# Reordering loads, transposes, stores and evacuations in the first three token tiles of a fused retention and gated-MLP kernel

## The chip, the cores and the metric

The kernel runs on one core of a Trainium2 chip. A core has five engines that run side by side and meet at semaphores: TensorE (PE in the profile; PEld is its weight load), VectorE (DVE), ScalarE (ACT), GpSimd (POOL) and SyncE (SP), which here only issues transfers. The metric is the device time of one execution in microseconds, as the median of several runs. The kernel before takes 303.74 us (three runs, 303.12 to 304.06). Times inside an execution come from a profile of it, whose span is 302.9 us.

## The reference

Two layers follow each other. The first is a retention layer: attention without softmax, whose scores decay with distance. Batch and heads are 8 each, the sequence has 576 tokens, the head dimension is 64. The second takes the 4608 tokens of 512 features through a layer of 2048.

```python
scores = q @ k.T / sqrt(64)                       # per batch and head
gamma  = 1 - 2 ** (-5 - head)
D[i, j] = gamma ** (i - j) if i >= j else 0
ret    = (scores * D) @ v                         # 8 x 8 x 576 x 64
x      = ret.transpose(0, 2, 1, 3).reshape(4608, 512)
h      = x @ w_in                                 # 4608 x 2048
g      = h * cos(h)
out    = g @ w_out                                # 4608 x 512, float32
```

## The kernel before

Tokens are handled in *pairs* of two 128-token tiles; there are 18 pairs of 256 tokens, numbered 0 to 17. For a pair the kernel loads q, k and v (1.5 MB), multiplies q and k by their decay factors and casts them (`prep`), turns them so that the head dimension lies on the partitions (`transposes`), and works out the retention in chunks: the part inside a chunk from masked scores, and the rest from a running state per head, which `states` sums up and `carry` moves on. The result goes from PSUM to `xT`, which feeds the second layer.

The second layer runs in ten *stages* n: widths 512, 256, 256, and then seven times 512 tokens. Stage 0 needs pairs 0 and 1, stage 1 pair 2, stage 2 pair 3, stage 3 pairs 4 and 5, stage 4 pairs 6 and 7. `mm1` is x @ w_in with the cosine, `mm2` is the second product. From stage 3 on, the second product is done with seven products in the place of eight (`mm2_seven`), for which sums of weights (`w_sums`) and of g (`g_sum`) are made on VectorE and GpSimd. The retention of later pairs is woven into the products of earlier stages.

Every load, DMA transpose and row store is issued from one queue, in program order:

```python
LD = 3                       # buffers for loaded q, k and v
def load(G, names="qkv", gate=None):
    for name in names:
        f = ld.tile([P, H, 2, D], F32, tag="f" + name, name=f"f{name}")
        for rows, ys, b, s0, cnt in parts:
            i = nc.sync.dma_start(f[rows, :, ys, :]..., src[b, :, s0 : s0 + cnt, :]...)
            if gate is not None:                  # the first transfer waits for a weight piece
                fence(i, gate, "weights first"); gate = None

def transposes(G, y, bank=None):
    qks, vb, qkT = tiles["a", G]
    if bank is None:                              # by DMA, from the same queue
        nc.sync.dma_start(qkT[:, y], qks[:, y]..., transpose=True)
        return
    ...                                           # pair 2: eight TensorE transposes
    nc.scalar.copy(qkT[:, y]..., ps[:, :, : HG * P])
```

The cast of v is put into the queue of one engine at the point where `prep` is called:

```python
def prep(G, y, engines=None, copy_v=None):
    ...
    scaled(eng, 0, tiles["fq", G], gq)            # eng is GpSimd unless told otherwise
    scaled(eng, 1, tiles["fk", G], gk)
    if copy_v is None:
        copy_v = nc.scalar.copy if G > 9 else nc.gpsimd.tensor_copy
    if copy_v:
        copy_v(vb[:, :, y], tiles["fv", G][:, :, y])
```

The store of each finished 128-token row tile s also drives the loading of later pairs. Up to stage 2 this goes through `bring` and a table, after that by a count:

```python
def mm2(n, tsi, et):
    ...
    if et == ET - 1:
        nc.scalar.copy(ot, ps)
        nc.sync.dma_start(out[s * P : (s + 1) * P, :], ot)
        feed(s)

loaded, prepared, transposed = 5, 4, 4
def bring(G):                                     # load ahead, prepare up to pair G, transpose
    while loaded < min(NP, G + LD, prepared // 2 + LD): load(loaded); loaded += 1
    while prepared < 2 * G + 2: prep_next()
    while transposed < prepared: transposes(...); transposed += 1

def feed(s):
    n, r = divmod(s - starts[S7] // P, 4)         # S7 = 3
    if n < 0:
        if s in when: bring(when[s])
        return
    while loaded < min(NP, prepared // 2 + LD): load(loaded); loaded += 1
    upto = starts[S7] // P + 12 + 4 * n + ((0, 0, 2, 4) if n else (0, 0, 2, 2))[r]
    while prepared < min(NG, upto): prep_next()
    while transposed < prepared: transposes(...); transposed += 1

when = {0: 3, 1: 4, 3: 5, 4: 6, 6: 7}             # a further bring(8) stands in stage 3
```

A retention ends with a copy of two halves from PSUM to `xT`. `done()` does both on ScalarE; `done(*both)`, with `both = (nc.scalar.copy, nc.vector.tensor_copy)`, does one on each engine. `begin` starts a pair's retention with its state part, `end` adds the rest and calls `done`. The second product of stages 0 to 2 is a list of matmuls into which such steps are put by index; stage 0's list before:

```python
todo = [(34 + 3 * i, w_sums(x, e, e + 4)) ...six of them...] + [
    (40, lambda: prep(2, 1, nc.vector, False)),
    (43, lambda: transposes(2, 0, "a")),
    (46, lambda: transposes(2, 1, "b")),
    (48, values2),                                # v of pair 2 and v_odd, both on ScalarE
    (50, lambda: at_once(*ready(2, states_bank=("n", "st")))),   # scores, states, masks
    (61, lambda: begin(2, ("n", "st"))),
    (64, lambda: end(both)),
]
```

Of the kernel before, what the change touches and what calls it, by code (L numbers as in the profile page):

```python
# [17 lines left out]
def kernel(  # L18
# [42 lines left out]
    LD = 3  # L61
# [49 lines left out]
    def half(x):  # L111
        return slice(x * HP, x * HP + HP)

    def load(G, names="qkv", gate=None):

        parts = []
        if G < FINE:
            t, end = G * 2 * P, (G + 1) * 2 * P
            while t < end:
                b, s0 = divmod(t, S)  # L120
                cnt = min(end - t, S - s0)
                p0 = (t - G * 2 * P) // 2
                parts.append((slice(p0, p0 + cnt // 2), slice(0, 2), b, s0, cnt))
                t += cnt
        else:
            for y in range(2):
                t0 = (2 * G + y) * P
                step = HP if (2 * G + y) % PER == MIX else P
                for p0 in range(0, P, step):
                    b, s0 = divmod(t0 + p0, S)  # L130
                    parts.append((slice(p0, p0 + step), slice(y, y + 1), b, s0, step))
        for name in names:
            src = {"q": q, "k": k, "v": v}[name]
            f = ld.tile([P, H, 2, D], F32, tag="f" + name, name=f"f{name}")
            for rows, ys, b, s0, cnt in parts:
                n = ys.stop - ys.start
                i = nc.sync.dma_start(  # L137
                    f[rows, :, ys, :].rearrange("p h r d -> p h (r d)"),
                    src[b, :, s0 : s0 + cnt, :].rearrange("h (p r) d -> p h (r d)", r=n),
                )  # L140
                if gate is not None:
                    fence(i, gate, "weights first")
                    gate = None
            tiles["f" + name, G] = f
# [28 lines left out]
            fv = tiles["fv", G]  # L173
            copy_v(vb[:, :, y], fv[:, :, y])  # L174

    def transposes(G, y, bank=None):
        qks, vb, qkT = tiles["a", G]
        if bank is None:
            nc.sync.dma_start(  # L179
                qkT[:, y], qks[:, y].rearrange("s m h d -> s (m h d)"), transpose=True  # L180
            )
            return
        ps = psum.tile([P, 2, 1024], BF16, tag=bank, name="tr")
        for m in range(2):
            for hg in range(HG):
                nc.tensor.transpose(
                    ps[:, m, hg * P : hg * P + P],
                    qks[:, y, m, 2 * hg : 2 * hg + 2, :].rearrange("s h d -> s (h d)"),
                    ident,
                )  # L190
        nc.scalar.copy(
            qkT[:, y].rearrange("p (m b) i -> p m (b i)", m=2), ps[:, :, : HG * P]
        )

    def key_transposes(G, bank):
        qks, vb, qkT = tiles["a", G]
# [27 lines left out]
    def blocks_of(G, y, hg):  # L224
        return slice(2 * hg, 2 * hg + 2) if G < FINE else slice(y * HG + hg, y * HG + hg + 1)

    def scores(G, banks="ab", idle=0, mid=lambda: None):

# [3 lines left out]
        for (y, ys), bank in zip(planes, banks):  # L234
            ps = psum.tile([P, 2, 2 * HG, HP], F32, tag=bank, name="sc")
            if idle:
                warm(ps[:, 0].rearrange("p b i -> p (b i)"), idle)
            ret = retp.tile([P, 2, 2 * HG, HP], BF16, tag="ret", name="ret")
            for u in range(2) if y is None else (y,):
                yq = slice(u, u + 1) if y is None else ys  # L240
                tiles["ret", G, u] = ret
                for hg in range(HG):
                    for x in range(2):
                        for he in range(2):
                            nc.tensor.matmul(  # L245
                                ps[half(x), he, blocks_of(G, u, hg), :],
                                lhsT=qkT[half(he), u, HG + hg, half(x)],
                                rhs=queries(G, he, hg, x, yq),
                                start=True,
                                stop=True,  # L250
                            )

            def masked(y=y, ps=ps, ret=ret):
                if y is None:
                    shape, by = [P, 2, 2 * HG, HP], tri.unsqueeze(1)
                    by = by.unsqueeze(1).to_broadcast(shape)
                    nc.vector.tensor_tensor(out=ret, in0=ps, in1=by, op=ALU.mult)  # L257
                    return
                shape = "p a (b r) i -> p (a b) (r i)"
                by = (mixed if G == 2 else tri2)[y].rearrange("p r i -> p (r i)")  # L260
                nc.vector.tensor_tensor(  # L261
                    out=ret.rearrange(shape, r=2),
                    in0=ps.rearrange(shape, r=2),
                    in1=by.unsqueeze(1).to_broadcast([P, H, P]),
                    op=ALU.mult,
                )

            masks.append(masked)
            if len(masks) == 1:
                mid()  # L270
        return masks

    def steps(G):
# [182 lines left out]
        for masked in masks:  # L456
            masked()

    def carry(G, bank):
        add, copy = states(due(G), bank)  # L460
        add()
        copy()

# [40 lines left out]
    def mm2(n, tsi, et):  # L504
# [11 lines left out]
        )  # L516
        if et == ET - 1:
            s = starts[n] // P + tsi
            ot = op.tile([P, DM], F32, tag="oabcd"[1 + s % 4], name="ot")
            nc.scalar.copy(ot, ps)  # L520
            nc.sync.dma_start(out[s * P : (s + 1) * P, :], ot)  # L521
            feed(s)

    E2 = ET // 2
    N2 = DM // 2
# [193 lines left out]
                    r0 = starts[n] + 256 + j * P  # L719
                    nc.sync.dma_start(out[r0 : r0 + P, N2 + c0 : N2 + c1], u22[:, j, c0:c1])  # L720

    loaded, prepared, transposed = 5, 4, 4
    open_ = []

    def begin(G, bank="m"):
        run, done = retention(G, bank)
# [10 lines left out]
        prep(prepared // 2, prepared % 2, **kw)  # L737
        prepared += 1

    def bring(G):  # L740

        nonlocal loaded, transposed
        while loaded < min(NP, G + LD, prepared // 2 + LD):
            load(loaded)
            loaded += 1
        while prepared < 2 * G + 2:
            prep_next()
        while transposed < prepared:
            transposes(transposed // 2, transposed % 2)
            transposed += 1  # L750

    def feed(s):

        nonlocal loaded, transposed
        n, r = divmod(s - starts[S7] // P, 4)
        if n < 0:
            if s in when:
                bring(when[s])
            return
        while loaded < min(NP, prepared // 2 + LD):  # L760
            load(loaded)
            loaded += 1
# [4 lines left out]
            transposes(transposed // 2, transposed % 2)  # L767
            transposed += 1

    when = {0: 3, 1: 4, 3: 5, 4: 6, 6: 7}  # L770

    G4 = 4
    fq4 = gp.tile([P, H, G4, D], F32, tag="gT", name="fq4")
# [121 lines left out]
    nc.gpsimd.tensor_copy(tiles["a", 1][1], tiles["fv", 1])  # L895
    w_dma += [load_w_in(e, e + 512) for e in (1024, 1536)]
    w_dma += [load_w_out(e, e + 4) for e in range(0, ET, 4)]
    load(2, gate=w_dma[5])
    load(3)
    load(4)  # L900
    plane = key_transposes(1, "m")
    plane(0)
    run, done = retention(0, ("n", "st"))
    run("cross", True)
    plane(1)
    masks1 = scores(1, mid=lambda: (run("own"), run("same"), done()))
    for masked in masks1:
        masked()
    add, copy = states(due(1), "m")
    add()  # L910
    copy()
# [7 lines left out]
        nc.gpsimd.tensor_copy(mixed[r], tri2[r])  # L919
        nc.gpsimd.memset(mixed[r][:QP, :, QP:], 0.0)  # L920
    prep(2, 0, copy_v=False)
    prepared = transposed = 6
    run1, done1 = retention(1, ("n", "st"))

    def values2():
        fv, vb = tiles["fv", 2], tiles["a", 2][1]
        nc.scalar.copy(vb, fv)
        nc.scalar.copy(v_odd[QP:HP], fv[QP:HP])

    late = []  # L930
    for n, w in enumerate(widths):

        if n in (0, 3):
# [1 line left out]
            if n == 3:  # L935
                order_.sort()
            else:
                order_[1:3] = order_[2:0:-1]
            blocks = [(et, h * 256, 256) for h, et in order_]
        else:  # L940
            m = 1024 // w
# [4 lines left out]
        for i, (et, c0, cw) in enumerate(blocks):  # L946
# [1 line left out]
            inside = {  # L948
                (0, 1): {
                    0: lambda: run1("own"), 1: lambda: run1("same", True),  # L950
                    2: lambda: (run1("cross"), done1()),
                },
                (3, 0): {3: lambda: carry(5, ("n", "st"))},
                (3, 2): {1: lambda: end()},
            }.get((n, i), {})
            mm1(n, et, c0, cw, banks[i], inside)
            if (n, i) == (S7, 1):
                late.pop()()
            if n >= S7:
                sums_after(n, i)  # L960

        G = (starts[n] + w) // (2 * P)
        if n == 0:
            todo = [
                (34 + 3 * i, lambda x=x, e=e: w_sums(x, e, e + 4))
                for i, (x, e) in enumerate((x, e) for x in (1, 6, 7) for e in (0, 4))
            ] + [
                (40, lambda: prep(2, 1, nc.vector, False)),
                (43, lambda: transposes(2, 0, "a")),
                (46, lambda: transposes(2, 1, "b")),  # L970
                (48, values2),
                (50, lambda: at_once(*ready(2, states_bank=("n", "st")))),
                (61, lambda: begin(2, ("n", "st"))),
                (64, lambda: end(both)),
            ]
        elif n == 1:
            todo = [
                (8, lambda: carry(3, "m")),
                (11, lambda: [masked() for masked in scores(3)]),
                (23, lambda: begin(3, "a")),  # L980
                (26, lambda: end(both)),
            ]
        elif n == 2:
            todo = [
                (8, lambda: carry(4, ("n", "st"))),
                (10, lambda: [masked() for masked in scores(4)]),
                (24, lambda: begin(4, "m")),
                (24, lambda: [masked() for masked in scores(5)]),
                (24, lambda: end()),
            ]  # L990
            late += [
                lambda: (begin(5, ("n", "st")), bring(8)),
            ]
        else:
            at = {}
# [72 lines left out]
```

## Time and profile before

| what | value |
|---|---|
| time, median of three runs | 303.74 us |
| span of the profiled execution | 302.9 us |
| TensorE matmul busy | 281.8 us (93%) |
| VectorE busy | 197.0 us (65%) |
| GpSimd busy | 183.4 us (61%) |
| ScalarE busy | 153.0 us (51%) |
| moved by DMA | 50.38 MB, mean 166 GB/s |

The profile has a page with the shares of each engine, and views of its trace: who waited for whom, a timeline for each engine, and windows with the busy time, the granted TensorE clock (PEclk, 1.00 is full) and the share of the DMA engines. A timeline line gives start in us, length, engine, source line, operation, the tile written and the tile read, how often, and in square brackets the idle time before it with what ended it. In the waits, `PE sc L245 <- DMA qkT<-qks: 4.1, 2, 3.4` says that TensorE's instruction writing `sc` at line 245 waited for the DMA that fills `qkT`, 4.1 us in all, twice, 3.4 us at most. Line 137 issues loads, 179 DMA transposes, 521 and 676 row stores. `h` is the first product, `o` the second, `sc` the scores, `st` the state sums, `ov` the retention.

### The profile page before, as it was taken

Reading aid. Unit: us, or ns where it says so; the run is one execution under the profiler, and the core shown is the slowest. Engines: PE = TensorE matmul, PEld = TensorE weight load, DVE = VectorE, ACT = ScalarE, POOL = GpSimd, SP = SyncE. Lnnn points to the kernel's source line nnn. Section 1 sums busy time; section 2 is a strip of 40 time slices with the busy share of each in tenths; the row PEclk is TensorE's granted clock in tenths of the full one; section 3 lists DMA queues with packets and bytes.
Section 4 is the critical chain, followed back from the end, with each engine's and each line's share of the span. In section 5 each row is a group of like instructions: output and inputs, shape, how many; then the busy total and the mean of one; then the engine's idle time right before and its main releaser. Section 6 shows DMA issues by size and latency. Waiting matters only on the chain.

```text
span 302.9 us, 8827 instructions
## 1 busy us (share of the span) xinstructions
PE 281.8 (93%) x3824; PEld 193.6 (64%) x3845; DVE 197.0 (65%) x253; ACT 153.0 (51%) x201; POOL 183.4 (61%) x163
## 2 busy tenths in 40 slices
PE   7779997889959899999999989999999999999995
PEld 2468653746636688746874677468647854784584
DVE  5654763472732798668886866787578757844863
ACT  5556435533404663466567644664665436534620
POOL 6780047774442426965798899289938903870483
PEclk9899999999987999999999999999999999999999
DMA  7999999999999999999989999998450220022013
GB/s 220 264 179 190 221 245 227 284 220 178 247 208 192 243 212 204 169 207 228 223 180 222 252 175 195 250 216 160 103 108 2 71 71 0 2 71 71 0 35 106
DMA packets 137718, 50.38 MB, mean 166 GB/s; under 512 B 107856, under 2 KB 136656, under 8 KB 137680
## 3 DMA queue, kind: packets, MB, share of 16 engines
q1 hardware_dynamic: 132912, 45.10, 73.6%
q0 software_dynamic: 4224, 4.19, 8.8%
q8 instruction: 30, 0.49, 0.7%
q10 hardware_dynamic: 544, 0.52, 0.5%
q14 instruction: 8, 0.07, 0.1%
HBM read 36.70 MB, written 9.44 MB: 152 GB/s over the span
## 4 chain that ended last, share of the span: by engine, by line
PE 78%; DMA 6%; SPq 6%; ACT 4%; DVE 2%; issue 2%; POOL 0%; DVEq 0%; ACTq 0%
PE h L493 38%; PE o L644 27%; PE o L510 5%; SPq L137 4%; PE ov L416 4%; DMA fk<-in_k_dram 3%; DMA fv<-in_v_dram 2%; PE sc L245 2%; PE st L318 1%; SPq L179 1%; ACT xT L442 1%; DMA qkT<-qks 1%; ACT cosh L501 1%; DVE ot L669 1%; SPq L521 0%
## 5 line engine op out<-in xcount | busy, mean ns | idle before, releaser
L571 POOL TENSOR_TENSOR gs<-gT 128x1024 bf16<-128x1024 bf16 x45 | 94.4, 2129 | 64.2 <-DVE gs L571 64.2
L493 PE MATMUL h<-xT,w_in_sb 128*128 128x256 bf16 (+1 forms) x756 | 127.5, 326 | 4.7 <-ACT xT L442 3.1
L502 DVE TENSOR_TENSOR gT<-h,cosh 128x1024 bf16<-128x1024 f32 x72 | 87.9, 1224 | 50.5 <-ACT cosh L501 50.5
L501 ACT ACTIVATE cosh<-h,half_pi 128x1024 f32<-128x1024 f32 x72 | 80.1, 1113 | 59.4 <-PE h L493 59.4
L493 PEld LDWEIGHTS <-w_in_sb 128*128 128x128 bf16 x768 | 74.8, 98 | 54.3 <-issue 4.4
L644 PEld LDWEIGHTS <-gs 128*128 128x128 bf16 x576 | 54.1, 98 | 6.7 <-POOL gs L571 0.2
L158 POOL TENSOR_TENSOR qks<-fq,gq 128x512 bf16<-128x512 f32 x31 | 32.9, 1061 | 32.5 <-DMA fq<-in_q_dram 19.7
L158 POOL TENSOR_TENSOR qks<-fk,gk 128x512 bf16<-128x512 f32 x34 | 36.9, 1086 | 7.7 <-DMA fk<-in_k_dram 6.0
L644 PE MATMUL o<-ws,gs 128*128 128x256 bf16 (+1 forms) x352 | 38.4, 268 | 0.0
L510 PE MATMUL o<-w_out_sb,gT 128*128 128x512 bf16 x119 | 30.0, 394 | 1.2 <-issue 1.0
L669 DVE TENSOR_TENSOR ot<-o,ot 128x512 f32<-128x512 f32 (+2 forms) x32 | 19.7, 621 | 11.2 <-PE o L644 10.4
L442 ACT CAST xT<-ov 128x512 bf16<-128x512 f32 x34 | 19.7, 632 | 13.3 <-PE ov L416 13.1
L644 PE MATMUL o<-w_out_sb,gT 128*128 128x256 bf16 x224 | 26.3, 273 | 0.0
L644 PE MATMUL o<-w_out_sb,gs 128*128 128x256 bf16 x224 | 25.9, 273 | 0.0
L644 PEld LDWEIGHTS <-gT 128*128 128x128 bf16 x224 | 21.5, 98 | 4.0
L349 ACT CAST sb<-s 128x768 bf16<-128x768 f32 (+2 forms) x16 | 10.5, 658 | 23.8 <-DVE s L341 21.3
L510 PEld LDWEIGHTS <-gT 128*128 128x128 bf16 x128 | 12.0, 100 | 13.6 <-issue 1.8
L261 DVE TENSOR_TENSOR ret<-sc,tri 128x1024 bf16<-128x1024 f32 x10 | 12.0, 1220 | 8.9 <-PE sc L245 8.8
L571 DVE TENSOR_TENSOR gs<-gT 128x1024 bf16<-128x1024 bf16 (+1 forms) x24 | 17.4, 755 | 0.4
L669 DVE TENSOR_TENSOR ot<-ot,o 128x512 f32<-128x512 f32 x14 | 9.6, 686 | 10.5 <-ACT ot L699 8.9
L257 DVE TENSOR_TENSOR ret<-sc,tri 128x1024 bf16<-128x1024 f32 x12 | 14.6, 1215 | 0.0
L174 POOL CAST vb<-fv 128x512 bf16<-128x512 f32 x14 | 8.6, 612 | 8.2 <-DMA fv<-in_v_dram 8.2
(77 smaller groups left out, 189.5 us busy)
## 6 DMA issues: line engine op xcount, KB each, us to landing
out_dram<-ot SPq DMA_DIRECT2D x35, 256.0 KB, 2.9
fq<-in_q_dram SPq DMA_DIRECT2D x25, 256.0 KB, 4.6
fk<-in_k_dram SPq DMA_DIRECT2D x23, 256.0 KB, 5.7
fv<-in_v_dram SPq DMA_DIRECT2D x23, 256.0 KB, 5.2
fk<-in_k_dram SPq DMA_DIRECT2D x4, 512.0 KB, 8.3
fv<-in_v_dram SPq DMA_DIRECT2D x4, 512.0 KB, 7.5
w_in_sb<-in_moe_w_in_dram POOLq DMA_DIRECT2D x4, 512.0 KB, 6.6
w_out_sb<-in_moe_w_out_dram POOLq DMA_DIRECT2D x4, 512.0 KB, 13.9
```

Of the source, the lines that this page charges most:

```text
L137: i = nc.sync.dma_start(f[rows, :, ys, :].rearrange("p h r d -> p h (r d)"), src[b, :, s0 : s0 + cnt, :].rearrange("h (p r) d -> p h (r d) ...
L158: eng.tensor_tensor(out=qks[:, y, m].rearrange("p (b a) d -> p a b d", a=2), in0=f[:, :, y, :].rearrange("p (a b) d -> p a b d", a=2), in1 ...
L257: nc.vector.tensor_tensor(out=ret, in0=ps, in1=by, op=ALU.mult)
L416: i = nc.tensor.matmul(outs[x][half(h % 2), yq, h // 2, :n], lhsT=lhsT, rhs=rhs, start=at not in begun, stop=left[at] == 0, skip_group_che ...
L442: (evacs or (evac, evac))[x](xT[:, x], outs[x])
L493: nc.tensor.matmul(ps[:, j, :], lhsT=w_in_sb[:, dg, (et + j) * P : (et + j + 1) * P], rhs=xT[:, dg, c0 : c0 + w], start=(dg == 0), stop=(d ...
L501: nc.scalar.activation(cosh, ps, ACTF.Sin, bias=half_pi, scale=1.0)
L502: nc.vector.tensor_mul(gT[:, et : et + m, c0 : c0 + w], ps, cosh)
L510: nc.tensor.matmul(ps, lhsT=gT[:, et, tsi * P : (tsi + 1) * P], rhs=w_out_sb[:, et, :], start=(et == 0), stop=(et == ET - 1),)
L571: i = (nc.vector if on_dve else nc.gpsimd).tensor_tensor(out=tiles["gs", n, x][:, e0:e1], in0=i0, in1=i1, op=op_)
L644: nc.tensor.matmul(dst[i], lhsT=lhs[:, e, j * P : (j + 1) * P], rhs=rhs[:, e, c0:c1], start=(x in (3, 4, 1, 7) and e == 0 and (i == 0 or l ...
L669: pend.append(lambda: nc.vector.tensor_tensor(out=out_, in0=in0, in1=in1, op=op_))
```

## The change

The change redoes the plan of stages 0 to 2. It has five parts.

1. Pairs 3 to 5 are prepared earlier on GpSimd (`early`), and their DMA transposes are put ahead of further loads: those of pair 3 before the v of pair 4 and the load of pair 5, those of pair 5 before the loads of 6 and 7.
2. Row stores are collected in a list and issued by `put` at chosen points, so that a transpose does not stand behind a store that is not ready. The first q load of pair 2 waits for an earlier weight piece than before.
3. Evacuations that stood one behind the other on ScalarE are spread: `done(*both)` also for pairs 0, 1, 4 and 5, VectorE for the second transposed half of pair 2, GpSimd for its v, VectorE for `v_odd`. Half of the weight sums move to stage 1.
4. The state sums of pairs 4 and 5 are made in one go in stage 2, and pair 5's retention begins and ends inside one block of stage 3.
5. The loads of the first stages are given by the plan (up to pair 8, with preparation and transposes up to 7), and the counters on which `feed` goes on in stage 3 are set to match. `feed` itself keeps its rule for stages from 3 on.

The core of the diff, with cuts:

```diff
-    def load(G, names="qkv", gate=None):
+    def load(G, names="qkv", gates=()):
...
-    def transposes(G, y, bank=None):
+    def transposes(G, y, bank=None, evac=nc.scalar.copy):
...
-    def carry(G, bank):
-        add, copy = states(due(G), bank)
+    def carry(Gs, bank):
+        add, copy = states([u for G in Gs for u in due(G)], bank)
...
             nc.scalar.copy(ot, ps)
-            nc.sync.dma_start(out[s * P : (s + 1) * P, :], ot)
-            feed(s)
+            stores.append(lambda: nc.sync.dma_start(out[s * P : (s + 1) * P, :], ot))
+            for step in plan.get(s, ()):
+                step()
...
-    loaded, prepared, transposed = 5, 4, 4
...
+    def early(G):
+        for y in range(2):
+            prep(G, y, copy_v=False)
+        for y in range(2):
+            nc.gpsimd.tensor_copy(tiles["a", G][1][:, :, y], tiles["fv", G][:, :, y])
+    def turned(G):
+        for y in range(2):
+            transposes(G, y)
+    def put(n=1):
+        for _ in range(n):
+            stores.pop(0)()
...
     def feed(s):
         n, r = divmod(s - starts[S7] // P, 4)
-        if n < 0:
-            if s in when:
-                bring(when[s])
-            return
         while loaded < min(NP, prepared // 2 + LD):
...
-    when = {0: 3, 1: 4, 3: 5, 4: 6, 6: 7}
+    plan = {
+        3: (put, lambda: early(5)),
+        4: (put, lambda: turned(5), lambda: load(6)),
+        5: (put, lambda: early(6), lambda: load(7)),
+        6: (put, lambda: turned(6)),
+        7: (put, lambda: load(8), lambda: early(7)),
+    }
+    loaded, prepared, transposed = 9, 16, 16
...
-    load(2, gate=w_dma[5])
+    load(2, gates=(w_dma[4], w_dma[5]))
     load(3)
-    load(4)
+    load(4, "qk")
...
-    masks1 = scores(1, mid=lambda: (run("own"), run("same"), done()))
-    for masked in masks1:
-        masked()
+    masks1 = scores(
+        1, mid=lambda masked: (masked(), run("own"), run("same"), done(*both))
+    )
+    masks1[1]()
...
     prep(2, 0, copy_v=False)
-    prepared = transposed = 6
+    nc.gpsimd.tensor_copy(tiles["a", 2][1], tiles["fv", 2])
+    early(3)
+    turned(3)
+    load(4, "v")
...
-                    2: lambda: (run1("cross"), done1()),
+                    2: lambda: (run1("cross"), done1(*both)),
                 },
-                (3, 0): {3: lambda: carry(5, ("n", "st"))},
-                (3, 2): {1: lambda: end()},
+                (3, 1): {0: lambda: begin(5, ("n", "st")), 2: lambda: end(both)},
             }.get((n, i), {})
             mm1(n, et, c0, cw, banks[i], inside)
             if (n, i) == (S7, 1):
-                late.pop()()                      # begin(5), bring(8)
+                turned(7)
...
-                (46, lambda: transposes(2, 1, "b")),
-                (48, values2),
-                (50, lambda: at_once(*ready(2, states_bank=("n", "st")))),
-                (61, lambda: begin(2, ("n", "st"))),
-                (64, lambda: end(both)),
+                (45, lambda: transposes(2, 1, "b", nc.vector.tensor_copy)),
+                (46, lambda: nc.vector.tensor_copy(v_odd[QP:HP], tiles["fv", 2][QP:HP])),
+                (46, lambda: (early(4), load(5), put(2), turned(4))),
+                (48, put),
+                (49, lambda: at_once(*ready(2, states_bank=("n", "st")))),
+                (60, lambda: begin(2, ("n", "st"))),
+                (63, lambda: end(both)),
...                                               # stage 2
-                (8, lambda: carry(4, ("n", "st"))),
-                (10, lambda: [masked() for masked in scores(4)]),
+                (5, lambda: carry((4, 5), ("n", "st"))),
+                (9, lambda: [masked() for masked in scores(4)]),
                 (24, lambda: begin(4, "m")),
                 (24, lambda: [masked() for masked in scores(5)]),
-                (24, lambda: end()),
+                (24, lambda: end(both)),
```

## The prediction

> **What bounds the kernel now.** I read the page first, then the waits, the matmul timeline, the windows, the load queue (SP) and ScalarE (ACT). TensorE is busy for 93% of the span and leads the chain that ended last, so only time in which it stands still or runs slowly can be won. The waits, in all, times and longest:
>
> ```profile
> PE sc L245 <- DMA qkT<-qks: 4.1, 2, 3.4
> PE h L493 <- ACT xT L442: 3.1, 3, 1.2
> PE st L318 <- ACT v_odd L928: 1.9, 1, 1.9
> PE h L493 <- DVE xT L442: 1.0, 2, 0.8
> ```
>
> The reader sees few and short waits, and the diff aims at just these. The largest, in the matmul timeline (start us, length, count, idle before):
>
> ```profile
> 85.02 0.30 PE L416 MATMUL ov<-qkT,sb 64*64 64x128 bf16 x4
> 88.72 1.07 PE L245 MATMUL sc<-qkT 64*64 64x128 bf16 x32 [3.40 <-DMA qkT<-qks]
> 89.55 1.10 PE L416 MATMUL ov<-ret,vb 64*64 64x128 bf16 x32
> ...
> 91.19 3.19 PE L510 MATMUL o<-w_out_sb,gT 128*128 128x512 bf16 x7 [0.33 <-issue]
> 94.17 1.79 PE L493 MATMUL h<-xT,w_in_sb 128*128 128x256 bf16 x12
> ```
>
> Not only 3.40 us are lost. The 7 matmuls of 91.19 take 0.456 us each; 20 like them take 4.48 us at 35.74, 0.224 each. The windows show why (PEclk, DMA share and GB/s are the last columns):
>
> ```profile
> 80.00:91.00 11.00, 7.29 (x138) 4.38 (x138) 5.44 (x6) 1.09 (x3) 5.25 (x6) 0.86 1.17 214
> 91.00:101.00 10.00, 9.12 (x124) 5.67 (x124) 3.81 (x6) 5.57 (x9) 4.46 (x5) 0.81 1.09 211
> 101.00:127.00 26.00, 25.37 (x451) 22.18 (x451) 21.17 (x28) 14.05 (x20) 14.31 (x11) 1.00 1.12 205
> ```
>
> The wait costs clock, and the DMA share never leaves full. Why the transposes were late, and what stands later in the same queue:
>
> ```profile
> 79.36 2.49 SPq L137 DMA_DIRECT2D fv<-in_v_dram  x2
> 81.96 4.68 SPq L179 DMA_TRANSPOSE qkT<-qks  x2
> ...
> 99.19 1.20 SPq L137 DMA_DIRECT2D fq<-in_q_dram  x2
> ...
> 110.53 1.18 SPq L137 DMA_DIRECT2D fq<-in_q_dram  x2
> ...
> 116.60 4.21 SPq L179 DMA_TRANSPOSE qkT<-qks  x2
> 120.90 0.53 SPq L676 DMA_DIRECT2D out_dram<-ot  x1
> ```
>
> Pair 5's transposes (81.96) stand behind pair 7's load. Loads of pairs 9 (99.19) and 10 (110.53) and pair 8's transposes are all issued before the first store of stage 3 (120.90). Last, ACT at the end of stage 3:
>
> ```profile
> 118.13 0.58 ACT L694 COPY ot<-o 128x512 f32<-128x512 f32 x1
> ...
> 123.53 1.13 ACT L174 CAST vb<-fv 128x512 bf16<-128x512 f32 x2
> 125.39 1.07 ACT L442 CAST xT<-ov 128x512 bf16<-128x512 f32 x2 [0.73 <-PE ov L416]
> 129.00 1.11 ACT L501 ACTIVATE cosh<-h,half_pi 128x1024 f32<-128x1024 f32 x1 [2.54 <-PE h L493]
> ```
>
> The cast at 123.53 is pair 10's v. It waits for nothing, because by the trace's DMA completions that v landed at about 120.5, only 3 us earlier. The xT copy behind it feeds stage 4.
>
> [...] its clock record has half clock for 6.8 us, from 87.9 to 94.8, after the 3.40 us wait. [...] here 8.0 us go by per 1.5 MB load from pair 6 on (completions 112.43 to 120.5, and 136.73 to 144.75). [...]
>
> **The change part by part, up to stage 3's products.**
> 1. Evacuations and v. Two copies in a row (1.30 at 21.6) become one on each engine (0.73): 0.6 us at the start. It is not added: pair 2's k lands at 41.2 whatever TensorE does, and GpSimd's product with it ends at 42.87, so the transposes stay near 43. Then ACT's row of two evacuations (2.11), store copy (0.59), v cast (1.06) and v_odd (1.04) is broken up: v goes to GpSimd, one evacuation and v_odd to VectorE. The states that began at 48.81 after a 1.86 wait can begin near 46.8. Gain 2.0; one more matmul covers the xT wait at 54.25: 0.2.
> 2. Pair 3's transposes are issued from about 49 instead of 57.18. The scores of 65.00 lose their 0.73.
> 3. Pair 5's transposes go ahead of loads 6 and 7. From completions of the same transfers (fk of pair 4 at 54.9, load 5 5.3 us, two transposes 2.4, a store 0.7) I get pair 3 at 57, pair 4 at 68, pair 5 at 72. Scores(5) come near 82.5, so 3.40 go. With them goes the half clock: 1.6 on the seven matmuls, 0.43 + 0.46 + 0.18 on scores and retention, 0.45 on the next twelve: 3.1.
> 4. State sums of pairs 4 and 5 together: the same 48 small matmuls in another place, 0. Pair 5's retention ends with both engines copying: 1.20 becomes 0.65, gain 0.55.
> 5. Stores held back, GpSimd's preparation brought forward: no cost on the path.
> Sum: 2.2 + 0.73 + 6.5 + 0.55 = 10.0 us. Stage 3's products begin at 101.6 instead of 111.6.
>
> **What it costs.** The new plan loads pair 8 and stops. Pairs 9 and 10 are asked for only when stage 3's first store is issued; before, the steps of stages 0 to 2 had loaded 9 and 10 and transposed 8. The changed queue then reads: store, load 9, load 10, transposes 8 and 9. By my ledger its last transfer ahead of that store ends near 104 (124.1 less two loads and a transpose pair, 19.5 us). That store can go when its copy ends: X = 118.7 - 10.0 = 108.7. For 4 to 5 us the DMA, the scarce resource, has nothing to do.
> Pair 10's v lands at X + 0.55 (store issue) + 1.0 (start) + 2 x 8.0 = X + 17.6. ACT still reaches its cast at X + 4.8 (123.53 - 118.71), waits there 12.8 us, casts until X + 18.2, and only then copies xT (1.07): X + 19.3. Stage 4's first matmul was at 127.2 = X + 8.5. So TensorE stands 10.8, say 11 us. Afterwards it runs at half clock [...] say 2.5.
> Pair 10's transposes: X + 17.6, transposes of 8 and 9 4.8, store 0.8, load 11 9.0, load 12 8.0, store 0.8, two transposes 2.4: X + 43.5. Their scores were at 153.63 = X + 34.9; pushed by 13.5 they come at X + 48.4 and wait for nothing. Pair 13's v (near X + 52.5, cast at X + 53) is just in time. From stage 5 on nothing differs.
> Net: -10.0 + 11.0 + 2.5 = +3.5 us; 303.7 + 3.5 = 307.2.
>
> **The rivals.**
> A. The gain stays: 294. For it: every wait it aims at is real, and the transposes have 9 us and more to spare. Against: it needs load 10 on chip by about X + 5, and its first byte is not asked for before X. I see no way around that in the built queues.
> B. ACT does not block, but scores(10) wait for their transposes: X + 43.5 against X + 34.9, 8.6 us, with 2.5 of clock: +1.1, 304.8. For it: the same late loads. Against: the cast stands ahead of the xT copy in ACT's order.
> C. An early wait remains: pair 5's transposes stand behind the row store of stage 1's first tile, or w_out is slowed by the q load that now starts one weight piece earlier. Margins are 10 us for the first, about 2 for the second (last piece lands at 36, first needed near 39.5). Half of the gain lost gives 311.
>
> **Range and chances.** The gain may be 8 to 11, the stall 9 to 13[...]: together 302.8 to 311.0 for 8 of 10. Faster by 2% (under 297.7) needs A: 0.06. Slower by 2% (over 309.8) needs a longer stall or C: 0.17. Within: 0.77.
>
> **What would show it.** Right: no wait of sc on qkT before 100 us; full clock from 80 to 100; stage 3's products near 101.6; the DMA idle for some us near 105; ACT waiting some 13 us for fv ahead of a vb cast; then matmul h waiting about 11 us for xT near 117 to 128, and half clock after it. Wrong: no such gap (A), or the gap at sc near 144 (B), or waits of sc, o or st before 90 us (C).

## The result, and the profile after

The changed kernel takes 312.12 us (median of four, 311.02 to 312.71) against 303.9 us, a ratio of 1.027 with a 95% interval from 1.022 to 1.031. It is slower by 2.7%. The prediction said 307.2 and a range up to 311.0. Ratios and intervals leave out executions that took over 1.5% longer than the fastest of their kernel (eight of twenty in experiment 6, two of four in experiment 7), while the medians count all. The span of the profiled execution went from 302.9 to 310.6 us, by 7.7 us.

The starts of the stages in the two matmul timelines show where those 7.7 us arise. *h* is a stage's first product, *o* its second.

| stage part | before, us | after, us | shift, us |
|---|---|---|---|
| o of stage 0 | 34.20 | 35.10 | +0.9 |
| h of stage 1 | 54.2 | 53.1 | -1.1 |
| h of stage 2 | 71.6 | 69.7 | -1.9 |
| h of stage 3 | 94.2 | 87.0 | -7.2 |
| o of stage 3 | 111.44 | 103.98 | **-7.5** |
| h of stage 4 | 127.01 | 133.29 | **+6.3** |
| o of stage 4 | 140.8 | 147.7 | +6.9 |
| h of stage 5 | 156.86 | 165.14 | +8.3 |
| h of stage 6 | 186.9 | 194.6 | +7.7 |
| h of stage 9 | 273.1 | 280.8 | +7.7 |

So the change does what it was made for, 7.5 us up to stage 3's second product. Within that one product it then loses 13.7 us (the stretch from o of stage 3 to h of stage 4 grew from 15.57 to 29.31). From stage 6 on nothing differs.

The waits of the changed kernel (line numbers have moved by a few):

```profile
PE ov L416 <- ACTq L428: 12.0, 1, 12.0
ACT vb L176 <- POOL qks L160: 12.0, 1, 12.0
...
PE h L493 <- DVE xT L442: 4.6, 6, 1.7
...
PE h L493 <- DMA w_in_sb<-in_moe_w_in_dram: 2.0, 2, 1.7
```

The two waits that the change aimed at, scores on `qkT` (4.1 us) and states on `v_odd` (1.9 us on ScalarE), are no longer among the large ones. A single stop of 12.0 us has come in. In the matmul timeline:

```profile
84.73 1.67 PE L510 MATMUL o<-w_out_sb,gT 128*128 128x512 bf16 x7 [0.16 <-issue]
...
92.72 2.47 PE L493 MATMUL h<-xT,w_in_sb 128*128 128x256 bf16 x21 [1.72 <-DVE xT L442]
...
129.11 0.64 PE L416 MATMUL ov<-ret,vb 64*64 64x64 bf16 x32 [12.04 <-ACTq L428]
...
129.90 3.60 PE L645 MATMUL o<-ws,gs 128*128 128x256 bf16 x16
```

The seven matmuls that took 3.19 us before (91.19) take 1.67 now: the early half clock is gone. At 129.11 is the new stop, and after it 16 matmuls take 3.60 us. Before, the same 16 took 1.92, and stage 4's first product followed at once:

```profile
125.26 1.92 PE L644 MATMUL o<-ws,gs 128*128 128x256 bf16 x16
127.01 13.98 PE L493 MATMUL h<-xT,w_in_sb 128*128 128x512 bf16 x62
```

The half clock has moved to the stop: the granted clock is 0.50 from 120.92 to 134.57, where the kernel before has 0.50 from 87.98 to 94.81. The windows agree (PE, PEld, DVE, ACT, POOL busy, then clock, DMA share and GB/s):

```profile
80.00:91.00 11.00, 10.12 (x174) 6.22 (x168) 6.48 (x7) 4.06 (x7) 6.87 (x8) 1.00 1.09 214
...
103.00:112.00 9.00, 9.00 (x146) 7.66 (x146) 8.36 (x12) 3.65 (x6) 5.64 (x3) 1.00 0.44 76
118.00:130.00 12.00, 0.89 (x49) 0.82 (x50) 0.00 (x0) 1.23 (x2) 12.00 (x14) 0.62 1.12 221
```

The first had a clock of 0.86 before. In the second, the DMA engines, whose share in the same stretch was 1.13 before, are more than half empty. In the third, TensorE works 0.89 us out of 12, ScalarE 1.23 and VectorE not at all; only GpSimd and the DMA are busy throughout. The load queue (SP) shows where the hole comes from:

```profile
101.13 3.62 SPq L181 DMA_TRANSPOSE qkT<-qks  x2
111.27 0.38 SPq L677 DMA_DIRECT2D out_dram<-ot  x1
111.70 1.19 SPq L139 DMA_DIRECT2D fq<-in_q_dram  x2
...
123.38 1.85 SPq L139 DMA_DIRECT2D fv<-in_v_dram  x2
```

After pair 7's transposes, which have landed at 106.6, there is nothing to issue until the first row store of stage 3 at 111.27. Load 9 begins behind that store; the two halves of load 10's v are issued from 123.38 on and land at 128.08 and 129.02 by the trace's DMA completions. ScalarE (ACT) meanwhile:

```profile
115.75 0.40 ACT L350 CAST sb<-carry 128x256 bf16<-128x256 f32 x1
128.18 0.62 ACT L176 CAST vb<-fv 128x512 bf16<-128x512 f32 x1 [12.03 <-POOL qks L160]
129.04 0.62 ACT L176 CAST vb<-fv 128x512 bf16<-128x512 f32 x1 [0.24 <-DMA fv<-in_v_dram]
130.02 1.07 ACT L442 CAST xT<-ov 128x512 bf16<-128x512 f32 x2 [0.36 <-PE ov L416]
```

ScalarE stands at the cast of pair 10's v. The profile names GpSimd's product as what released it, and not the load. The product ends at 128.08 and the first half of the load lands at 128.08 too, so this line alone doesn't say which of them was waited for; the experiments do. TensorE stops earlier than the xT copy would force it to. Line 428 of the program puts an instruction into ScalarE's queue that the next matmul of the retention has to wait for (`ACTq L428`, 12.04 us), and that instruction too stands behind the cast.

### The profile page after: what moved, and what is told of

Read it like the earlier page. It is cut to its first block, busy times and chain, and to the rows that moved or that the text cites. A ratio compares the mean times of both kernels' runs of the same rounds, so it can differ in the third digit from the quotient of the medians.

```text
span 310.6 us, 8820 instructions
## 1 busy us (share of the span) xinstructions
PE 279.1 (90%) x3822; PEld 191.8 (62%) x3845; DVE 202.2 (65%) x259; ACT 147.5 (47%) x193; POOL 184.9 (60%) x164
## 4 chain that ended last, share of the span: by engine, by line
PE 79%; DMA 7%; POOL 5%; DVE 3%; issue 3%; ACT 1%; SPq 1%; DVEq 0%; POOLq 0%; ACTq 0%
PE h L493 39%; PE o L645 26%; PE o L510 7%; PE ov L416 3%; DMA w_in_sb<-in_moe_w_in_dram 3%; DMA fk<-in_k_dram 3%; POOL qks L160 2%; POOL gs L572 2%; PE st L318 2%; DMA fv<-in_v_dram 2%; PE sc L245 2%; DVE xT L442 1%; SPq L139 0%; DVE ret L261 0%; DVE gT L502 0%
## 5 line engine op out<-in xcount | busy, mean ns | idle before, releaser
L645 PEld LDWEIGHTS <-gs 128*128 128x128 bf16 x576 | 54.9, 99 | 7.3 <-POOL gs L572 0.2
L645 PE MATMUL o<-ws,gs 128*128 128x256 bf16 (+1 forms) x352 | 40.0, 275 | 0.0
L510 PE MATMUL o<-w_out_sb,gT 128*128 128x512 bf16 x117 | 27.9, 379 | 1.0 <-issue 0.8
L442 ACT CAST xT<-ov 128x512 bf16<-128x512 f32 x30 | 17.3, 618 | 11.3 <-PE ov L416 11.1
L416 PE MATMUL ov<-ret,vb 64*64 64x64 bf16 (+1 forms) x576 | 9.4, 205 | 12.0 <-ACTq L428 12.0
L416 PEld LDWEIGHTS <-vb 64*64 64x64 bf16 x576 | 7.2, 110 | 13.6 <-ACTq L428 12.2
L176 ACT CAST vb<-fv 128x512 bf16<-128x512 f32 x16 | 9.0, 616 | 12.3 <-POOL qks L160 12.0
```

The lines of the kernel that those rows point to most:

```text
L416: i = nc.tensor.matmul(outs[x][half(h % 2), yq, h // 2, :n], lhsT=lhsT, rhs=rhs, start=at not in begun, stop=left[at] == 0, skip_group_che ...
L442: (evacs or (evac, evac))[x](xT[:, x], outs[x])
L510: nc.tensor.matmul(ps, lhsT=gT[:, et, tsi * P : (tsi + 1) * P], rhs=w_out_sb[:, et, :], start=(et == 0), stop=(et == ET - 1),)
L645: nc.tensor.matmul(dst[i], lhsT=lhs[:, e, j * P : (j + 1) * P], rhs=rhs[:, e, c0:c1], start=(x in (3, 4, 1, 7) and e == 0 and (i == 0 or l ...
```

## The experiments

Two theories of the 12 us. **Theory 1**: pair 10's v comes late, because its load is asked for only behind stage 3's first row store, and ScalarE takes its queue in order. **Theory 2**: GpSimd, which the profile names, is late with its products. For the small losses ahead of stage 3, and later for what bounds the repaired kernel, further theories stand in the expectations. Ratios are to the kernel before on the same chip, with 95% intervals; the medians of different chips differ by up to 1%. A trace is of one execution; where that was far from the median, the text says so.

**1. Ask for loads 9 and 10 earlier.** In the changed kernel, after pair 7's transposes:

```diff
                 turned(7)
+                load(9)
+                load(10)
+                loaded = 11
```

> The changed kernel with one addition: loads of pairs 9 and 10 are queued right behind pair 7's transposes, not at stage 3's first store. Theory 1 (v of pair 10 lands late, ScalarE waits for it): the DMA is busy until about 106.5 with pair 7's transposes, two loads take 16.2, so v of pair 10 lands near 122.7 and not at 128.9; ScalarE reaches its cast at 116.2, so the wait falls from 12.0 to about 6.5 us and the time to about 306. Theory 2 (GpSimd, which the profile names, holds the cast: its sums and preparations end only at 127): nothing about GpSimd's order changes, the wait stays near 12 and the time at 312.

Measured: 306.58 us, ratio 1.006 (1.004 to 1.009), span 304.4. The stop fell from 12.0 to 6.7 us. The first half of pair 10's v now lands at 121.68, and the cast follows:

```profile
121.78 1.29 ACT L176 CAST vb<-fv 128x512 bf16<-128x512 f32 x2 [6.87 <-POOL qks L160]
```

The order of GpSimd's work was not changed, only that of the loads, so its lateness followed from theirs: theory 2 falls, and 5.3 of the 12 us came from the hole in the DMA. The rest of the wait is still there, at the same cast.

**2. Pair 10's v on GpSimd.** The changed kernel with one threshold:

```diff
-            copy_v = nc.scalar.copy if G > 9 else nc.gpsimd.tensor_copy
+            copy_v = nc.scalar.copy if G > 10 else nc.gpsimd.tensor_copy
```

> The changed kernel with pair 10's v cast on GpSimd instead of ScalarE, loads as late as before. Theory 1: the 12 us wait of the retention goes, as nothing in ScalarE's queue waits for the late v; but the late loads show up at the next place, the scores of pair 10: due near 146.7, their transposes land at 153.2, so a wait of 6 to 7 us on qkT, with half clock after it; time about 306. If the late loads are harmless by themselves and only the cast's place was wrong: no such wait, about 297.

Measured: 310.92 us, ratio 1.017 (1.008 to 1.026), span 304.9. The trace is of the fastest of the four executions (306.86 us; the others took 310.65 to 311.72). In it the 12 us stop is gone and stage 4 begins at 118.35, 8.7 us earlier than before the change. But the late loads then stop others. The waits of this kernel:

```profile
PE sc L245 <- DMA qkT<-qks: 4.0, 2, 3.5
...
PE h L493 <- DVE gT L502: 3.7, 2, 2.1
```

Scores of pair 10 wait for their transposes, as the rival B of the prediction has it, for 3.5 us and not for 8.6. The h of stage 4 waits 2.1 us for the product with the cosine, because VectorE is held for 3.67 us at the sum of two g tiles ahead of it (more of this in experiment 3 and at the end); that of stage 5 waits 1.6 us, behind a wait of 3.67 us of ScalarE for a later v. The cast in ScalarE's queue is thus what turned the late load into the stop; the late load itself costs even without it.

**3. Both.** The two edits above in one kernel.

> Both edits: loads of pairs 9 and 10 queued behind pair 7's transposes, and pair 10's v cast on GpSimd. Theory 1: no wait over 3 us on TensorE after stage 2; the transposes of pair 10 land near 149 for scores due near 147, so 0 to 2 us there; time 297 to 299, below the kernel before by about 5 us. Theory 2 (GpSimd is the bound): a wait of several us stays, 303 or more.

Measured: 307.34 us, ratio 1.007 (1.004 to 1.011), span 305.1. **A miss**: stage 4 begins 7.3 us earlier than before the change, and by stage 6 this kernel is 2.2 us behind the kernel before. These lines carry the reasons:

```profile
129.24 3.79 DVE L572 TENSOR_TENSOR gs<-gT 128x1024 bf16<-128x1024 bf16 x1
```

```profile
131.86 0.62 POOL L176 CAST vb<-fv 128x512 bf16<-128x512 f32 x1
133.11 4.21 POOL L572 TENSOR_TENSOR gs<-gT 128x1024 bf16<-128x1024 bf16 x2 [0.63 <-DVE gs L572]
```

```profile
159.54 1.28 ACT L176 CAST vb<-fv 128x512 bf16<-128x512 f32 x2 [3.67 <-DMA fv<-in_v_dram]
```

The sum of two g tiles on VectorE takes 3.79 us, where the kernel before has 0.69 for the same sum (136.53). It ends at 133.03, 0.55 us after GpSimd ends an unbroken row of preparations (from 117.09 to 132.48), inside which it now begins. The row stands at nearly the same time in the changed kernel (116.83 to 131.08); what moved is VectorE's sum, which comes at 129.24 without the stop and at 143.44 with it, where it takes 0.69. The product h waits 2.25 us behind it. Then, in stage 5, pair 13's v lands at about 160, and ScalarE stands 3.67 us for it ahead of a cosine, with h waiting 3.42 us behind: the first fault once more, one stage later.

**4. The kernel before with the hole alone.** No load beyond pair 8 until stage 3's first store; nothing else of the change is in it:

```diff
-        while loaded < min(NP, G + LD, prepared // 2 + LD):
+        while loaded < min(9, G + LD, prepared // 2 + LD):
```

> The kernel before with one suspected cause put in: no load beyond pair 8 until stage 3's first store, all else as it was. Theory 1: that store can go at about 118.7, two loads then take 17.6, v of pair 10 lands near 136; ScalarE, which reaches its cast at 123.5, waits about 12 to 13 us, then half clock costs 2.5: about 318. Theory 2: GpSimd still has pair 8 done early, so a delay of at most 5 us: 305 to 309.

Measured: 319.18 us, ratio 1.048 (1.043 to 1.054), span 318.0. The late loads alone make the kernel before 14 us slower by the medians and 15 by the spans, with the same stop:

```profile
PE ov L416 <- ACTq L428: 13.8, 1, 13.8
```

That shows theory 1 from the other side. It also gives the sum of the change, in spans: about 15 us of harm from the loads, less some 7 us of gain.

**5. The two small losses ahead of stage 3.** The changed kernel with stage 0's block order of before, and stage 3's first weight sum behind the xT copy in VectorE's queue:

```diff
-                w_sums(3 + i % 2, i // 2 * 4, i // 2 * 4 + 4)
+                for j in ((), (0, 1), (2,), (3,))[i]:
+                    w_sums(3 + j % 2, j // 2 * 4, j // 2 * 4 + 4)
...
-                order_ = [(h, 4 * b) for h, b in zip((0, 0, 0, 1, 1, 1, 0, 1), (0, 1, 2, 0, 1, 2, 3, 3))]
+                order_[1:3] = order_[2:0:-1]
```

> The changed kernel with two small parts of its early stages taken back or mended: the order of the first product's blocks in stage 0 as before (the third weight piece is then needed two blocks later), and the first weight sum of stage 3 on VectorE only after the xT copy. If these two explain most of the 2.5 us that the early gain fell short: TensorE's waits on w_in (1.66 and 0.36) go, stage 0's second product begins near 34.0 instead of 35.1, the xT wait of 1.72 in stage 3 becomes about 1.05, and stage 3's products begin near 102.5 instead of 103.98. If the late k of pair 2 (landing at 42.05) is the real limit, the first gives nothing after 44 us and only 0.7 remains. The 12 us wait stays.

Measured: a single execution of 311.73 us, span 309.7. Stage 0's second product starts at 34.2 (35.1 in the changed kernel), stage 3's at 102.8 (103.98). The stop at ScalarE then takes 12.9 us where it took 12.0: of the 1.2 us gained ahead of it, it takes 0.9 back. As this kernel is a little shifted in time, its waits also name the other releaser:

```profile
ACT vb L176 <- DMA fv<-in_v_dram: 13.1, 2, 12.8
```

The same wait, "POOL" in one kernel and "DMA" in the other: the last of two that end together is all that such a line tells.

**6. Casts of v one row store later.** The kernel of experiment 1, and in it ScalarE's casts of pairs from 10 on are put into its queue at the next row store instead of at `prep`:

```diff
+        if copy_v is None and G > 9:
+            fv = tiles["fv", G]
+            casts.append(lambda: nc.scalar.copy(vb[:, :, y], fv[:, :, y]))
+            return
...                                               # at the start of the next feed
+        while casts:
+            casts.pop(0)()
```

> The changed kernel with loads of pairs 9 and 10 queued behind pair 7's transposes, and ScalarE's v casts of pairs 10 to 17 put one row store later in its queue, behind the xT copies; no cast moves to GpSimd. Theory 1 in its wider form (every late v that stands in ScalarE's queue ahead of what TensorE needs costs a wait): the 12 us wait and the 3.4 us wait of stage 5 in the run with both edits both go; the transposes of pair 10 still cost about 2; about 301. If instead the DMA as a whole is the bound, the time lost moves to another wait and stays at 305 or more.

Measured: 303.89 us, against 306.01 for the kernel before on that chip, ratio 0.990 (0.986 to 0.993). The first version that beats the kernel before, by 0.7% in the medians. Compared with experiment 1, only the places of some casts in one queue differ; that is worth 0.9% by the medians (306.58 against 303.89) and 1.6% by the ratios (1.006 against 0.990).

**7. Pair 8 prepared and turned early as well.** Experiment 6, with pair 8's preparation and transposes between loads 9 and 10, as the kernel before had pair 8 ready before stage 3's first store:

```diff
                 load(9)
+                for y in range(2):
+                    prep(8, y, copy_v=False)
+                turned(8)
                 load(10)
-                loaded = 11
+                loaded, prepared, transposed = 11, 18, 18
+                casts.append(lambda: nc.gpsimd.tensor_copy(tiles["a", 8][1], tiles["fv", 8]))
```

> As the run with deferred casts, and pair 8 prepared on GpSimd in its hole near 94 to 104 us with its transposes between loads 9 and 10, as the kernel before had them. Theory: in the run with both edits four transposes held the queue for 8.7 us while GpSimd prepared pairs 8 and 9, and the DMA share fell to 0.82; with pair 8 done early the queue does not stop, pair 10's transposes land 2 us earlier and their wait goes; 299. If GpSimd's sums are pushed late by this, VectorE or the products wait: 302 or more.

Measured: 303.92 us, ratio 0.985 (0.976 to 0.994); it can't be told from experiment 6. In its trace, of an execution of 305.36 us, the transposes delay load 10 (their issue takes the queue from 112.83 to 117.41, ahead of it), whose v lands from 126.95 on, and ScalarE waits 7.04 us for it, with h waiting 5.0 us for g behind it. That execution lies above the median, and no trace says whether the others wait as long.

**8. All of it.** Experiment 7 with the two repairs of experiment 5, and with pair 10's transposes put ahead of load 12:

```diff
-        while loaded < min(NP, prepared // 2 + LD):
+        while loaded < min(NP if (n, r) not in ((0, 1), (0, 2)) else 12, prepared // 2 + LD):
```

> As the run before it, with pair 10's transposes ahead of load 12, the stage 0 block order of before, and the first weight sum after the xT copy. Each should be worth what it was alone: 1 to 1.5 us together in the first stages, up to 1 us at pair 10; 297 to 298, clearly below the kernel before.

Measured: 305.78 us, ratio 0.999 (0.996 to 1.001), span 301.1. **A miss** by some 2%. The trace is of an execution of 303.08 us. What remains in its waits:

```profile
ACT vb L174 <- DMA fv<-in_v_dram: 5.4, 2, 4.9
...
PE h L497 <- DVE gT L506: 3.1, 1, 3.1
```

Two readings were open now. Either it was again one late v in ScalarE's queue, or the DMA is simply full and any order only moves the wait about.

**9. Pair 10's v out of ScalarE's way.** Experiment 8, with load 10 ahead of pair 8's transposes, and pair 10's v on GpSimd (the delayed casts begin with pair 11):

```diff
-        if copy_v is None and G > 9:
+        if copy_v is None and G > 10:
...
                 load(9)
+                load(10)
                 for y in range(2):
                     prep(8, y, copy_v=False)
                 turned(8)
-                load(10)
```

> c3_all with two things changed: load 10 is issued ahead of pair 8's transposes again, and pair 10's v is cast on GpSimd, so that no late v stands ahead of stage 4's cosine in ScalarE's queue. Theory 1 (in-order queues): what remained of the stall was ScalarE's 4.9 us wait for that v and the 3.1 us wait of h on gT behind it; both go, the span falls by about 3 us to 298, and the time to about 1.5% below the kernel before on the same chip. Theory 2 (the DMA is full, and order only moves the wait): the time stays within 1% of the kernel before, and a wait of about 3 us turns up elsewhere, at scores of pair 8 or 10 on qkT or at g sums on GpSimd.

Measured: 299.22 us (297.84 to 303.11, six runs) against 305.8 us on the same chip, ratio **0.978 (0.973 to 0.982)**, span 296.8. That is faster than both kernels. Its matmul timeline:

```profile
116.62 1.92 PE L650 MATMUL o<-ws,gs 128*128 128x256 bf16 x16
118.38 13.98 PE L497 MATMUL h<-xT,w_in_sb 128*128 128x512 bf16 x64
```

The last sums of stage 3 take 1.92 us, as in the kernel before, where the clock was 1.00 (125.26 to 127.20), and all 64 matmuls of stage 4's first product follow without a gap. Stage 3's second product starts at 101.58, 9.9 us before the kernel before, and 6.2 us of that are still there at stage 9 (266.9 against 273.1). The DMA moves the same bytes; an order of them that gains 6 us exists, so the full DMA was not what took the gain away in experiment 8.

**10. Experiment 9 without the two early repairs.**

```diff
-                for j in ((), (0, 1), (2,), (3,))[i]:
-                    w_sums(3 + j % 2, j // 2 * 4, j // 2 * 4 + 4)
+                w_sums(3 + i % 2, i // 2 * 4, i // 2 * 4 + 4)
...
-                order_[1:3] = order_[2:0:-1]
+                order_ = [(h, 4 * b) for h, b in zip((0, 0, 0, 1, 1, 1, 0, 1), (0, 1, 2, 0, 1, 2, 3, 3))]
```

> d1_v10_gpsimd_first with stage 0's block order and the place of stage 3's first weight sum as the changed kernel has them. The two repairs brought stage 3's products forward by 2.4 us (103.98 against 101.6). If what is gained early now stays, this kernel is about 2 us slower than d1 (span 299, time about 1.5% below before); if stages 4 and 5 are again held by something late, it ends where d1 ends (span 297).

Measured: 301.67 us, ratio 0.986 (0.980 to 0.993), span 296.4. The span of experiment 9 is 296.8, so in the traces the 1.5 us which this kernel is behind at stage 3 (103.05 against 101.58) are made up. But its trace is of the fastest of its five executions (298.48 us; the others took 301.11 to 302.37), and the ratios put it 0.9% behind, with intervals that overlap. Inconclusive as to the end. As to the start, 0.6 of the 1.5 us is the xT wait (1.65 against 1.05). Stage 0's block order gives 0.15 us here: stage 0's second product starts at 33.84, and at 33.69 in experiment 9. The remaining 0.7 lies between there and h of stage 1, and experiment 11, which keeps both repairs, has it too.

**11. Experiment 9 with pair 10's v back on ScalarE**, one row store later:

```diff
-        if copy_v is None and G > 10:
+        if copy_v is None and G > 9:
```

> d1_v10_gpsimd_first with one thing put back: pair 10's v is cast on ScalarE, one row store later, as in c3_all; load 10 stays ahead of pair 8's transposes. If the engine of the cast is what freed the 4 us between c3 and d1, ScalarE waits for that v again and the span returns to about 300. If the order of load 10 was, v lands by about 124, ScalarE hardly waits and the span stays at 297.

Measured: 301.56 us, ratio 0.985 (0.980 to 0.991), span 298.5. ScalarE waits 3.9 us again, and h 1.7 us for g behind it. Of the two steps from experiment 8 to 9, the order of load 10 gave the larger part (0.999 to 0.985, intervals apart), and the engine of the cast perhaps 0.7% more (0.985 to 0.978, intervals that overlap). The three ratios come from three chips, each against the kernel before on its own.

## Why the prediction was right and where it was wrong

**The mechanism holds.** Most signs that the prediction named are in the trace: no large wait of scores before 100 us, full clock from 80 to 100 (1.00), a hole in the DMA near 105 (106.6 to 111.3, share 0.01), ScalarE standing at a cast of v for some 13 us (12.03), TensorE standing 11 us (12.04), half clock after it (0.50 up to 134.57). Two came out otherwise: stage 3's products begin at 103.98 and not near 101.6, and what stands is a matmul of the retention that waits for ScalarE's instruction, not h that waits for xT. The v was to land 17.6 us after the end of the row's copy; that copy ended at 111.25, and the second half of v landed at 129.02, 17.8 us later.

**The sum was too small by 4.2 us** (3.5 predicted, 7.7 in the spans). By its terms:

| term | predicted, us | measured, us |
|---|---|---|
| gain up to stage 3's second product | 10.0 | 7.46 |
| stop and half clock, to the end of stage 4's first product | 13.5 | 13.74 + 0.63 |
| after that | 0 | 0.8 |
| net | +3.5 | +7.7 |

- *The failed step is the gain*: 10.0 us were said and 7.46 measured. Two places of the sum are too large.

  Steps 3 and 4 were to give 7.05 us together and gave 5.5. The wait of scores and its half clock did go, but both steps took no account of what stands in VectorE's queue. Step 4 said that pair 5's end costs 0.65 us in place of 1.20; the wait is 1.72. VectorE's queue says why:

```profile
90.13 1.23 DVE L502 TENSOR_TENSOR gT<-h,cosh 128x1024 bf16<-128x1024 f32 x1 [3.20 <-ACT cosh L501]
91.27 0.76 DVE L547 TENSOR_TENSOR w_out_sb<-w_out_sb 128x1024 bf16<-128x1024 bf16 x1
91.95 0.72 DVE L442 CAST xT<-ov 128x512 bf16<-128x512 f32 x1
```

  The half of xT that was moved to VectorE stands behind a g product and a weight sum there. ScalarE's half of this copy ends at 91.56 and VectorE's at 92.67; the product behind it begins at 92.72, with the later of the two. A second wait of the same kind, 0.58 us at 86.98 behind the masks, was not foreseen either. Both come back in the traces of experiments 1 to 3 and 10, which keep this plan: 0.57 to 0.58 us, and 1.65 to 2.06. With the weight sum put behind the copy (experiments 5, 8, 9 and 11) the longer of the two is 1.05.

  Step 1 said 2.2 us up to stage 1; it was 1.1. From stage 0's second product to h of stage 1 the change does gain 2.0 (20.0 us before, 18.0 after), but that second product starts 0.9 us late. In this trace TensorE waits 1.66 us for a piece of `w_in` that lands at 24.56. Stage 0's block order, changed in lines the prediction passed over, asks for that piece two blocks sooner. Yet experiment 1 has the same order, the piece lands at 23.10, and the wait is short:

```profile
24.61 10.65 PE L493 MATMUL h<-xT,w_in_sb 128*128 128x256 bf16 x96 [1.66 <-DMA w_in_sb<-in_moe_w_in_dram]
```

```profile
23.14 10.65 PE L493 MATMUL h<-xT,w_in_sb 128*128 128x256 bf16 x96 [0.17 <-DMA w_in_sb<-in_moe_w_in_dram]
```

  The first line is of the changed kernel, the second of experiment 1. In experiments 2, 3 and 10, with the same order, TensorE does not wait for that piece at all. So the order lets a late piece be felt, and why it was late in this execution is not shown. Up to stage 3's second product experiments 1 to 3 run the plan of the changed kernel; they reach it at 102.73, 102.74 and 104.24, a gain of 8.7, 8.7 and 7.2 us. The 10.0 is in none of them. Experiment 9 reaches 101.58, where the prediction put it, but with order and weight sum put back.
- *Step 2 held.* From h of stage 1 to h of stage 2 the changed kernel gains 0.8 us (0.73 predicted).
- *Stop and clock.* 12.0 us stood where 11 was said. It begins before pair 7's own matmuls, at the instruction of line 428 in ScalarE's queue, and not at the first product of stage 4. The lost clock comes to 1.7 us on the 16 sums (3.60 against 1.92) and at most 0.6 on stage 4's first product; 2.5 was said, the author's estimate.
- *After that.* The prediction had nothing differ from stage 5 on. A gap of 1.57 us in front of the last state sums at 163.16, where there was 0.20 before, comes in; the trace gives "issue" as its cause, and a wait of 1.10 us that the kernel before had in stage 5 is 0.65. Experiment 9 has the gap too, with 1.47 us. Why it grows stays open.

**The rivals.** A (the gain stays) falls for the kernel as built. B was right that the late transposes would cost even without ScalarE's block, 3.5 us (experiment 2). C was right that early waits would remain, and gave 311, but it named two others. As to the range, the three errors all point the same way, and the gain came out below the 8 to 11 that the range allowed. With the 2.5 us of half clock, the bounds of gain and stall add up to 304.2 to 311.2, not to 302.8 to 311.0; the measured 312.12 lies above both.

**Where the gain went.** Experiments 1, 4 and 9 settle it: the gain is real (9.9 us at stage 3 with the two repairs), and the loads asked for late, acting through the order of ScalarE's queue, turn it into a loss. Of these, 3.6 us are gone again by stage 6 in experiment 9. Its trace shows new waits of 0.34 and 0.32 us for VectorE in stage 3, the gap of 1.47 us in stage 4 and 0.77 us for g in stage 5; what causes them was not tested.

## What to carry to other kernels

When a plan moves transposes ahead of loads, follow each load that was moved back to the engine instruction that first needs it, and look what stands behind that instruction in its queue: in the changed kernel one late transfer held ScalarE for 12.03 us at a cast, and TensorE stood 12.04 us for an instruction queued behind it. A cast of data that may come late belongs at a later place in the queue, or on an engine with nothing urgent behind it. Before a copy is split over two engines, look at what stands in both queues at that moment: here the half on VectorE made one wait longer, 1.72 us in place of 1.20.

## What the runs showed of the hardware that was not expected

VectorE's sum of two bf16 g tiles in SBUF (128x1024) took 3.79 us in experiment 3 and 3.67 in experiment 2. The thirteen traces hold 299 such sums. The 225 that began with no GpSimd instruction under way took 0.68 to 0.69 us each. The other 74 began during one and took 0.77 to 3.79. Of these, 71 ended 0.54 to 0.56 us after GpSimd's unbroken row of instructions did, however many were left in the row; three got in between two instructions of a row and took 1.05 to 1.33. VectorE's g products in the same stretch of experiment 3, of which one input comes from PSUM, kept their 1.22 to 1.23 us.

The sum thus mostly lasted through the whole rest of GpSimd's row, in experiment 3 from 129.24 past the row's end at 132.48, and not through one instruction of 1.05 us. No run changed only GpSimd's part, so that the row is what held the sum is argued from these times and not shown.
